# A retention kernel with two MLPs: token groups of two chunks of each sequence, shared decays, and an order of operations from a table

## Chip, cores and metric

The kernel runs on one core of a Trainium2 chip. The metric is the device time of one execution in microseconds (us), lower is better. PE is the matrix engine (PEld its weight loads), DVE the vector engine, ACT the scalar engine, POOL the GpSimd engine, SP the engine whose queue issues the DMAs here.

## What is computed

A retention layer (attention with a decaying state) for 2 sequences of 768 tokens and 8 heads of 64, then two MLPs of 512 x 2048 x 512 on the 1536 tokens, the first with a rational activation, the second with SiLU:

```python
gamma = 1.0 - 2.0 ** (-5.0 - np.arange(H))
for t in range(S):
    state = gamma[None, :, None, None] * state + np.einsum('bhd,bhe->bhde', k[:, :, t], v[:, :, t])
    y[:, :, t] = np.einsum('bhd,bhde->bhe', q[:, :, t], state) / np.sqrt(D)
x = y.transpose(0, 2, 1, 3).reshape(B * S, H * D)
h = x @ w_in; h2 = h * h
g = (a[0] + a[1] * h + a[2] * h2 + a[3] * h2 * h) / (1.0 + np.abs(b[0]) * np.abs(h) + np.abs(b[1]) * h2 + 1e-6)
x = g @ w_out
h = x @ w_in2; g = h / (1.0 + np.exp(-h))
out = g @ w_out2
```

The weights arrive as 64-bit words. The kernel makes of each a float32 (the double is put together from its two halves by integer operations) and splits it into a high and a low part, and does likewise with the activations, so that three matmuls (high x high, low x high, high x low) stand for one.

## The kernel before, in words

*Attention.* A sequence is 6 chunks of 128 tokens; `attention(c, ...)` (line 395) lists the work of one of 12 chunks. It loads kT, qT, v, k (256 KB each); multiplies k by the decay of its tokens (`kn`, POOL); computes scores (`sc`, line 417) in two PSUM banks, multiplies them by the mask on DVE (`am`); scales q by the decays `gq`, a load of 256 KB for each chunk that has a state before it (POOL, line 441); computes the growth of the state (`grow`, line 450) and the output (`outs`: line 462 within the chunk, line 472 with the state). DVE adds the growth to the state (`bd`, two buffers taken in turn, 64 x 256 twice); ACT writes the high part of the output, `xh`, and DVE the low part, `xl`. The sequence of a chunk is `divmod(c, NCI)`: chunks 0 to 5 are the first sequence, 6 to 11 the second.

*Groups.* Four chunks make a group of 512 tokens (`GT`), so there are three groups. The MLPs work on a group: 16 slices of 128 of the 2048 hidden features, two slices to a pair of weights. `use_order` (line 177) lists the uses of the pairs, 24 for the first layer and 24 for the second; a step is one slice of one group, so there are 96 steps, 48 in each layer. A step has 12 matmuls of 128x512 into a bank h (`mm_in`, line 508), the activation on ACT and DVE (11 operations in the first layer, two in the second), the split of its result into `gh` (ACT) and `gl` (POOL up to step `glp` = 21, DVE behind that), and 12 matmuls into four banks acc (`mm_out`, line 558).

*Weights.* `weights(u)` (line 332) prepares the pair of use u: four units (512 KB of raw 64-bit words each, 256 KB as float32). Of each, ACT does two activations (`wt<-raw`, `raw<-raw,par`), DVE two integer operations (line 308, `wt<-wt,raw` and `wt<-raw,wt`), ACT the high part (line 370), and POOL or DVE the low part (line 375: POOL for the first layer up to use `lop1`, for the second up to use `lop2` = 24, which is none). Four slots hold pairs, six from the end of attention on. 16 pairs are prepared from raw words and 8 brought back, as float32, from copies written to DRAM (`spill`).

*Order.* The code first lists all operations with engine, duration and rank (`op`, line 58). `Flow.order` (line 73) then plays them through engine by engine, the ready one of least rank first, and emits them in that order. The ranks come from the numbers in `R`. So every engine's queue is fixed when the kernel is built; on the chip an engine waits for the semaphores of what it needs and does nothing else meanwhile. All DMAs are issued by SP, in order.

Of the kernel before, what the change touches and what calls it, by code (L numbers as in the profile page):

```python
# [1 line left out]

# [10 lines left out]
ALU = mybir.AluOpType  # L13

P = 128
RING = 4
LATE = 2
GT = 512
UNIT = 512
R = {'T0': 321.15, 'tau0': 7.46, 'tau1': 48.5, 'c0': -178.03, 'dc': 40.95, 'conv': 16.72, 'half': 117.82, 'absl': -3.34, 'raw': 149.99, 'ret': 721.79, 'spl': 159.79, 'hi': 3.19, 'lo': -120.86, 'inn': 327.86, 'later': 56.09, 'split': 40.22, 'out': 153.78, 'evac': -230.82, 'qload': 1.4, 'scl': 120.62, 'sc': 68.71, 'am': -21.97, 'gr': 164.55, 'av': -289.58, 'bd': -408.25, 'xh': -7.59, 'xl': 65.69, 'glp': 21, 'lop1': 16, 'lop2': 24, 'scp': 0, 'ps': 18, 'ksc': 24.5, 'ka': 0, 'late': 15, 'mid': 4, 'pev': -94.54, 'pld': 38.1, 'wm': 11, 'mk': -0.34, 'ck': 14.22, 'g2': (1, 0, 2), 'lw': -276.76}  # L20
# [4 lines left out]

class Cell:


# [14 lines left out]
class Flow:  # L43
# [6 lines left out]


    TAIL = {"pe": 0.19, "act": 0.15, "dve": 0.113, "pool": 0.103, "host": 0.0}
    ISSUE, FIRST = 0.43, 2.0

# [3 lines left out]
    def op(self, eng, dur, rank, emit, reads=(), writes=(), port=False):  # L58
        after = []
        for c in reads:  # L60
            after += c.writers
        for c in writes:
            after += c.writers + c.readers
        o = Op(eng, dur, rank, emit, list(dict.fromkeys(after)), port)
        for c in reads:
            c.readers.append(o)
        for c in writes:
            c.writers, c.readers = [o], []
        o.index = len(self.ops)
        self.ops.append(o)  # L70
        return o

    def order(self):
        free = {e: 0.6 for e in (*self.TAIL, "sync")}
        cands, done = {e: [] for e in free}, []
        port = 0.0
        landed = 0.0
        for o in self.ops:
            if not o.waits:
                cands[o.eng].append(o)  # L80
        while True:
            best = None
            for e, cs in cands.items():
                if cs:
                    at = max(free[e], min(max(o.ready, port) if o.port else o.ready for o in cs))
                    if best is None or at < best[0]:
                        best = (at, e)
            if best is None:
                break
            at, e = best  # L90
            o = min(
                (o for o in cands[e] if (max(o.ready, port) if o.port else o.ready) <= at + 1e-9),
                key=lambda o: (o.rank, o.index),
            )
            cands[e].remove(o)
            o.start = at
            if e == "sync":
                free[e] = at + self.ISSUE
                landed = max(at + self.FIRST, landed) + o.dur
                end = landed + 0.1  # L100
            else:
# [12 lines left out]
        return done  # L114
# [3 lines left out]
def retention_two_mlps(  # L118
# [18 lines left out]
    B, NCI = qt.shape[:2]  # L137
# [85 lines left out]
    def at_chunk(c):  # L223
        return 5.5 * c if c < CPG else T0 + R["c0"] + R["dc"] * (c - CPG)

# [48 lines left out]
    bank = {n: Buf(n, [P, GT], F32, psum) for n in ("a0", "a1", "acc0", "acc1", "acc2", "acc3", "h0", "h1")}  # L274

# [56 lines left out]
    def weights(u):  # L332
        (l, p), s, old = loads[u]
        sl = slots[s]
        need = at_step[2 * u]
        for half in range(2):
            w = w_dram[l][half].bitcast(I32)
            nm = "io"[half]
            for un in range(2):
                rank = need - R["conv"] + R["half"] * half + un  # L340
# [5 lines left out]
                else:  # L346
# [8 lines left out]
                    dma(need - R["raw"] + half, 1.32, dst, src.rearrange("(c p) f -> p c f", p=P), [], [rh, rl])  # L355
# [26 lines left out]

    def attention(c, s_banks, o_banks):
        b, ci = divmod(c, NCI)
# [113 lines left out]
    def step(s, l, g, u, j, first, last, part):  # L498
# [43 lines left out]
        for m in range(4):  # L542
# [44 lines left out]
            elif last:  # L587
# [9 lines left out]
                r0 = g * GT + m * P  # L597
# [120 lines left out]
```

## Time and profile before

| | |
|---|---|
| time, median of 3 runs | 618.96 us (618.27 to 619.92) |
| profiled execution: its own time | 618.69 us |
| its span, first to last instruction | 616.9 us |
| mean granted TensorE clock | 0.986 |
| PE busy | 587.8 us, 95% |
| DVE busy | 441.3 us, 72% |
| ACT busy | 388.9 us, 63% |
| POOL busy | 98.2 us, 16% |
| moved by DMA | 71.34 MB |

One execution was recorded. The span is cut into 40 slices on the page: PE is at 6 to 9 tenths in the first third and at 9 or more behind it, DVE at 8 or 9 tenths from the third slice to the 27th and at 1 to 5 behind, and the DMA engines are full in the first three slices. Busy time of PE is no measure of its rate, as its instructions overlap; counts of matmuls in a window are.

### The profile page before, as it was taken

To read this page: it belongs to the slowest core of one execution; us is meant where nothing else is said; L and a number is where in the kernel's file an instruction comes from. 1 tells how busy PE (TensorE), PEld (TensorE's weight loads), DVE (VectorE), ACT (ScalarE), POOL (GpSimd) and SP (SyncE) were. 2 spreads that over 40 slices of the span, in tenths; PEclk is the share of its full clock that TensorE was granted. 3 is DMA by queue.
4 is the path that set the end of the run, shared out by engine and by line. 5 is a ranking of instruction groups with operands and counts; after the bars stand their busy time and mean duration, and the time that the engine had idled before them with its cause. 6 is when DMAs were issued, how large, how long until landed. Compare 5 with 4: busy or idle time off the path is not lost.

```text
span 616.9 us, 8056 instructions
## 1 busy us (share of the span) xinstructions
PE 587.8 (95%) x2950; PEld 477.2 (77%) x2950; DVE 441.3 (72%) x674; ACT 388.9 (63%) x657; POOL 98.2 (16%) x80
## 2 busy tenths in 40 slices
PE   6689989999989999999999999999999999999997
PEld 6577767677768788788787877877888888888886
DVE  1788998999999999999999898985424133332321
ACT  1568878898899787879788588874333132432222
POOL 1753654455443100000000000000000000000000
PEclk8988989999989999999999999999999999999999
DMA  8996774442342211004201545684122000020001
GB/s 282 384 359 210 269 255 146 156 128 75 100 150 86 70 52 35 34 1 142 98 0 52 165 156 188 208 265 162 51 86 64 6 0 26 23 73 1 0 2 68
DMA packets 34088, 71.34 MB, mean 116 GB/s; under 512 B 3712, under 2 KB 3712, under 8 KB 34048
## 3 DMA queue, kind: packets, MB, share of 16 engines
q1 hardware_dynamic: 34048, 70.82, 34.8%
q8 instruction: 23, 0.38, 0.2%
q14 instruction: 17, 0.14, 0.1%
HBM read 58.22 MB, written 12.58 MB: 115 GB/s over the span
## 4 chain that ended last, share of the span: by engine, by line
PE 32%; DVE 15%; ACT 9%; DMA 6%; issue 3%; ACTq 0%; DVEq 0%; SPq 0%
PE acc L558 17%; PE h L508 15%; DMA raw<-in_moe_w_out_dram 3%; DMA raw<-in_moe_w_in_dram 3%; DVE wt L308 2%; DVE s L308 2%; ACT r L293 2%; DVE gl L301 2%; DVE u L308 2%; DVE r L308 1%; DVE t L308 1%; ACT w L293 1%; ACT wt L293 1%; ACT s L293 1%; ACT gh L293 1%
## 5 line engine op out<-in xcount | busy, mean ns | idle before, releaser
L508 PE MATMUL h<-xh,ih 128*128 128x512 f32 x384 | 153.6, 400 | 7.1 <-DVE s L308 5.9
L508 PE MATMUL h<-xh,il 128*128 128x512 f32 x384 | 150.8, 393 | 0.3 <-DVE il L375 0.3
L508 PE MATMUL h<-xl,ih 128*128 128x512 f32 x384 | 150.5, 392 | 0.0
L301 DVE TENSOR_TENSOR gl<-w,gh 128x512 fp32r<-128x512 f32 x48 | 33.2, 691 | 104.4 <-ACT gh L293 104.4
L293 ACT ACTIVATE gh<-w 128x512 fp32r<-128x512 f32 x48 | 30.3, 631 | 104.4 <-PE acc L558 104.4
L508 PEld LDWEIGHTS h<-xh,ih 128*128 128x128 f32 x384 | 72.7, 189 | 30.2 <-DVE s L308 12.7
L508 PEld LDWEIGHTS h<-xh,il 128*128 128x128 f32 x384 | 72.5, 189 | 17.1 <-DVE il L375 1.6
L508 PEld LDWEIGHTS h<-xl,ih 128*128 128x128 f32 x384 | 72.7, 189 | 14.3
L558 PE MATMUL acc<-gh,oh 128*128 128x512 f32 x192 | 76.3, 397 | 0.0
L558 PE MATMUL acc<-oh,gh 128*128 128x512 f32 x192 | 74.8, 390 | 0.8 <-DVE xl L301 0.8
L558 PE MATMUL acc<-gl,oh 128*128 128x512 f32 x192 | 75.0, 391 | 0.0
L558 PE MATMUL acc<-gh,ol 128*128 128x512 f32 x192 | 75.0, 391 | 0.0
L558 PE MATMUL acc<-ol,gh 128*128 128x512 f32 x192 | 74.7, 389 | 0.0
L558 PE MATMUL acc<-oh,gl 128*128 128x512 f32 x192 | 74.7, 389 | 0.0
L308 DVE SCALAR_TENSOR_TENSOR wt<-raw,wt 128x512 int32<-128x512 int32 x64 | 53.6, 845 | 0.3
L308 DVE SCALAR_TENSOR_TENSOR wt<-wt,raw 128x512 int32<-128x512 int32 x64 | 46.9, 744 | 9.1 <-ACT raw L293 8.1
L293 ACT ACTIVATE wt<-raw 128x512 f32<-128x512 f32 x64 | 42.5, 667 | 16.7 <-DMA raw<-in_moe_w_in_dram 8.4
L293 ACT ACTIVATE raw<-raw,par 128x512 int32<-128x512 uint32 x64 | 48.4, 761 | 5.0 <-DMA raw<-in_moe_w_in_dram 3.3
L308 DVE SCALAR_TENSOR_TENSOR s<-s,par,h 128x512 f32<-128x512 f32 x66 | 48.9, 743 | 0.9
L308 DVE SCALAR_TENSOR_TENSOR w<-w,h 128x512 f32<-128x512 f32 x48 | 33.0, 687 | 19.2 <-ACT w L293 18.4
L558 PEld LDWEIGHTS acc<-oh,gh 128*128 128x128 f32 x192 | 36.0, 187 | 8.7 <-DVE xl L301 1.2
L558 PEld LDWEIGHTS acc<-gh,oh 128*128 128x128 f32 x192 | 36.3, 189 | 7.9
(88 smaller groups left out, 921.6 us busy)
## 6 DMA issues: line engine op xcount, KB each, us to landing
raw<-in_moe_w_in_dram SPq DMA_DIRECT2D x32, 512.0 KB, 4.0
raw<-in_moe_w_out_dram SPq DMA_DIRECT2D x32, 512.0 KB, 3.9
spill<-wt SPq DMA_DIRECT2D x32, 256.0 KB, 4.8
wt<-spill SPq DMA_DIRECT2D x32, 256.0 KB, 2.7
kT<-in_kt_dram SPq DMA_DIRECT2D x12, 256.0 KB, 5.6
qT<-in_qt_dram SPq DMA_DIRECT2D x12, 256.0 KB, 4.7
vn<-in_v_dram SPq DMA_DIRECT2D x12, 256.0 KB, 5.2
kn<-in_k_dram SPq DMA_DIRECT2D x10, 256.0 KB, 5.5
```

The costliest lines, as they stand in the source:

```text
L293: lambda: nc.scalar.activation(out=out_, in_=in_, func=func, **kw),
L301: op(eng, dur, rank, lambda: e.tensor_tensor(out=out_, in0=in0, in1=in1, op=alu), reads, writes, port)
L308: lambda: nc.vector.scalar_tensor_tensor(out=out_, in0=in0, scalar=scalar, in1=in1, op0=op0, op1=op1),
L508: nc.tensor.matmul(h.t, sl.t[w][:, ws], x[g].t[:, c, :], start=(n == 0), stop=(n == 3 * KD - 1))
L558: nc.tensor.matmul(a.t, a1, a2, start=(first and n == 0), stop=(last and n == 2))
```

## The change

- Chunk c is now sequence `c % 2`, chunk `c // 2`: a group of 512 tokens is two neighbouring chunks of each sequence. The rows of the output are put in place when they are stored.
- The decays `gq` of a chunk index are loaded once and used for both sequences (`shared`).
- Each sequence has one state buffer, updated in place.
- The order of emission is read from a packed table, `ORDER`, in place of the playing through; the ranks have no effect any more. It holds one number for each of 2124 operations.
- Of the numbers in `R`, those that still choose something have changed so: `glp` 21 to 25 (gl on POOL up to step 25), `lop2` 24 to 30 (the low parts of the second layer's pairs used at 24 to 29 on POOL), `ka` 0 to 4 (k of chunks 0 to 3 is multiplied by its decay on ACT, one activation per head, instead of on POOL), `ps` 18 to 17 (up to which step the reciprocal is kept in the bank h), `lop1` 16 to 15 and `late` 15 to 20 (no difference in what is loaded where).

The table's text, the rest of the numbers, and edits that change a rank alone are left out here:

```diff
--- before.py
+++ after.py
@@ -1,4 +1,8 @@
+import base64
+import zlib
 from contextlib import ExitStack
+
+import numpy as np
 
 import concourse.bass as bass
 import concourse.tile as tile
@@ -17,14 +21,60 @@
 LATE = 2
 GT = 512
 UNIT = 512
-R = {'T0': 321.15, 'tau0': 7.46, ... 'glp': 21, 'lop1': 16, 'lop2': 24, 'scp': 0, 'ps': 18, ... 'ka': 0, 'late': 15, 'mid': 4, ... 'wm': 11, ... 'g2': (1, 0, 2), 'lw': -276.76}
+R = {'lw': -463.92, 'T0': 689.59, 'tau0': 13.93, ... 'glp': 25, 'lop1': 15, 'lop2': 30, 'scp': 0, 'ps': 17, ... 'ka': 4, 'late': 20, 'mid': 4, ... 'wm': 11, ... 'g2': (1, 0, 2), ... 'rhalf': 125.38}
 L_SCALE = 2.0**-29 * (1.0 - 2.0**-16)
 L_BIAS = -0.5 + 7.5 * 2.0**-16
 W_SCALE = 2.0**-112
 
 
+ORDER = (
...
+)
+
+
...
@@ -47,11 +97,6 @@
 
 
 
-
-
-    TAIL = {"pe": 0.19, "act": 0.15, "dve": 0.113, "pool": 0.103, "host": 0.0}
-    ISSUE, FIRST = 0.43, 2.0
-
     def __init__(self):
         self.ops = []
 
...
@@ -71,46 +118,12 @@
         return o
 
     def order(self):
-        free = {e: 0.6 for e in (*self.TAIL, "sync")}
-        cands, done = {e: [] for e in free}, []
-        port = 0.0
-        landed = 0.0
-        for o in self.ops:
-            if not o.waits:
-                cands[o.eng].append(o)
-        while True:
-            best = None
-            for e, cs in cands.items():
-                if cs:
-                    at = max(free[e], min(max(o.ready, port) if o.port else o.ready for o in cs))
-                    if best is None or at < best[0]:
-                        best = (at, e)
-            if best is None:
-                break
-            at, e = best
-            o = min(
-                (o for o in cands[e] if (max(o.ready, port) if o.port else o.ready) <= at + 1e-9),
-                key=lambda o: (o.rank, o.index),
-            )
-            cands[e].remove(o)
-            o.start = at
-            if e == "sync":
-                free[e] = at + self.ISSUE
-                landed = max(at + self.FIRST, landed) + o.dur
-                end = landed + 0.1
-            else:
-                free[e] = at + o.dur
-                end = at + o.dur + self.TAIL[e]
-            if o.port:
-                port = at + o.dur
-            o.end = end
-            for f in o.feeds:
-                f.ready = max(f.ready, end)
-                f.waits -= 1
-                if not f.waits:
-                    cands[f.eng].append(f)
-            done.append(o)
-        assert len(done) == len(self.ops)
+        places = np.frombuffer(zlib.decompress(base64.b85decode("".join(ORDER))), np.uint16)
+        assert sorted(places) == list(range(len(self.ops)))
+        done = [self.ops[n] for n in places]
+        for n, o in enumerate(done):
+            o.place = n
+        assert all(o.place < f.place for o in done for f in o.feeds)
         return done
 
 
...
@@ -380,8 +396,10 @@
                 op("pool" if on_pool else "dve", 1.23 if on_pool else 0.6, rank + R["lo"], lo, [wt, ch], [cl], True)
 
 
+    shared = {}
+
     def attention(c, s_banks, o_banks):
-        b, ci = divmod(c, NCI)
+        ci, b = divmod(c, B)
         g, o = divmod(c, CPG)
         rank = at_chunk(c)
         more, grows = ci > 0, ci < NCI - 1
@@ -433,15 +451,15 @@
                 port=False,
             )
 
-        old = bd[(c - 1) % 2]
+        old = new = bd[b]
         if more:
 
-            gq = load(0.5, gqs, decays[ci - 1])
+            gq = shared[ci] if ci in shared else load(0.5, gqs, decays[ci - 1])
+            shared[ci] = gq
             eng = "dve" if c < R["scp"] else "pool"
             tt(eng, rank - R["scl"], qT.t[:], qT.t[:], gq.t[:], ALU.mult, [gq], [qT])
 
 
-        new = bd[c % 2]
         st, xo = bank[o_banks[0]], bank[o_banks[1]]
 
         def grow():
@@ -488,7 +506,7 @@
                 if not more:
                     act(rank + R["bd"], new.t[js, :, js], sv[js], AF.Copy, [st], [new], True, n=HP * D)
                 else:
-                    tt("dve", rank + R["bd"], new.t[js, :, js], sv[js], old.t[js, :, js], ALU.add, [st, old], [new], n=HP * D, port=False)
+                    tt("dve", rank + R["bd"], new.t[js, :, js], sv[js], new.t[js, :, js], ALU.add, [st], [new], n=HP * D, port=False)
         cols = slice(o * P, (o + 1) * P)
         hi, lo = xh[g].t[:, :, cols], xl[g].t[:, :, cols]
         act(rank + R["xh"], hi, heads(xo.t), AF.Copy, [xo], xh[g].chunk[o], True)
@@ -594,7 +612,8 @@
                     [a],
                     [o],
                 )
-                r0 = g * GT + m * P
+                ci, b = divmod(g * CPG + m, B)
+                r0 = (b * NCI + ci) * P
                 op(
                     "sync",
                     0.8,
```

## Rows read from the trace of the kernel before

**Rows 1.** The page, part 1: busy us, share of the span, instructions

```profile
PE 587.8 (95%) x2950; PEld 477.2 (77%) x2950; DVE 441.3 (72%) x674; ACT 388.9 (63%) x657; POOL 98.2 (16%) x80
```

**Rows 2.** The chain that ended last: start us, us, what

```profile
589.55 5.44 PE acc L558 x24
...
597.71 15.65 PE acc L558 x69
```

**Rows 3.** Windows of line 508: stretch, us, PE busy (matmuls); clock, DMA share, GB/s

```profile
36.00:180.00 144.00, 59.18 (x238) 0.96 0.54 178
...
300.00:420.00 120.00, 61.00 (x253) 1.00 0.46 147
```

**Rows 4.** The same for line 558 alone (`mm_out`)

```profile
36.00:180.00 144.00, 48.16 (x192) 0.96 0.54 178
...
300.00:420.00 120.00, 60.18 (x255) 1.00 0.46 147
```

**Rows 5.** PE in order of time: start, us, line, tiles, count [idle before <-releaser]

```profile
30.44 0.32 PE L462 MATMUL h<-u,vn 128*64 128x128 f32 x1 [1.98 <-DVE xl L301]
...
35.78 0.50 PE L508 MATMUL h<-xh,ih 128*128 128x512 f32 x1 [0.55 <-DVE xl L301]
...
66.03 0.69 PE L450 MATMUL a<-vn,kn 128*64 128x64 f32 x16
66.55 1.04 PE L462 MATMUL a<-am,vn 128*64 128x128 f32 x16
67.52 1.16 PE L472 MATMUL a<-qT,bd 128*128 128x128 f32 x8
...
75.49 1.16 PE L417 MATMUL a<-qT,kT 64*128 64x128 f32 x16
```

**Rows 6.** Windows: stretch, us; busy (x) PE PEld DVE ACT POOL; clock, DMA, GB/s

```profile
15.00:30.00 15.00, 9.52 (x144) 8.11 (x144) 11.09 (x17) 9.26 (x18) 11.16 (x9) 1.00 1.02 381
30.00:45.00 15.00, 14.01 (x120) 11.53 (x120) 13.24 (x19) 8.33 (x15) 8.84 (x8) 0.89 1.03 377
...
60.00:180.00 120.00, 111.73 (x646) 88.15 (x646) 112.43 (x163) 101.52 (x174) 59.77 (x45) 0.97 0.48 158
...
300.00:420.00 120.00, 117.27 (x508) 94.36 (x507) 109.95 (x177) 96.32 (x163) 0.00 (x0) 1.00 0.46 147
```

**Rows 7.** DVE in order of time, late: start us, us, what

```profile
392.93 0.68 DVE L301 TENSOR_TENSOR gl<-w,gh 128x512 fp32r<-128x512 f32 x1
393.53 0.69 DVE L375 TENSOR_TENSOR il<-wt,ih 128x512 fp32r<-128x512 f32 x1
```

**Rows 8.** DVE in order of time

```profile
9.22 1.29 DVE L301 TENSOR_TENSOR am<-a,msk 128x512 f32<-128x512 f32 x2 [7.80 <-DMA msk<-in_consts_dram]
...
27.69 1.65 DVE L308 SCALAR_TENSOR_TENSOR wt<-raw,wt 128x512 int32<-128x512 int32 x1
...
29.71 0.67 DVE L301 TENSOR_TENSOR xl<-h,xh 128x512 fp32r<-128x512 f32 x1
```

**Rows 9.** POOL in order of time

```profile
24.36 1.27 POOL L375 TENSOR_TENSOR il<-wt,ih 128x512 fp32r<-128x512 f32 x1
...
27.07 1.72 POOL L375 TENSOR_TENSOR il<-wt,ih 128x512 fp32r<-128x512 f32 x1
28.76 1.72 POOL L301 TENSOR_TENSOR qT<-qT,gq 128x512 f32<-128x512 f32 x1
```

**Rows 10.** ACT in order of time

```profile
6.55 0.29 ACT L293 ACTIVATE u<-u,par 128x1 f32<-128x1 f32 x1 [3.76 <-PE h L625]
14.88 0.60 ACT L293 ACTIVATE xh<-h 128x512 fp32r<-128x512 f32 x1 [8.04 <-PE h L462]
...
18.66 0.38 ACT L293 ACTIVATE bd<-h 64x256 f32<-64x256 f32 x1 [2.35 <-PE h L450]
```

**Rows 11.** The page, part 5: busy us, mean ns | idle before, releaser

```profile
L308 DVE SCALAR_TENSOR_TENSOR wt<-raw,wt 128x512 int32<-128x512 int32 x64 | 53.6, 845 | 0.3
L308 DVE SCALAR_TENSOR_TENSOR wt<-wt,raw 128x512 int32<-128x512 int32 x64 | 46.9, 744 | 9.1 <-ACT raw L293 8.1
```

More of the change, by code (lines that the diff above doesn't have):

```diff
@@ L19 @@
 UNIT = 512
-R = {'T0': 321.15, 'tau0': 7.46, 'tau1': 48.5, 'c0': -178.03, 'dc': 40.95, 'conv': 16.72, 'half': 117.82, 'absl': -3.34, 'raw': 149.99, 'ret': 721.79, 'spl': 159.79, 'hi': 3.19, 'lo': -120.86, 'inn': 327.86, 'later': 56.09, 'split': 40.22, 'out': 153.78, 'evac': -230.82, 'qload': 1.4, 'scl': 120.62, 'sc': 68.71, 'am': -21.97, 'gr': 164.55, 'av': -289.58, 'bd': -408.25, 'xh': -7.59, 'xl': 65.69, 'glp': 21, 'lop1': 16, 'lop2': 24, 'scp': 0, 'ps': 18, 'ksc': 24.5, 'ka': 0, 'late': 15, 'mid': 4, 'pev': -94.54, 'pld': 38.1, 'wm': 11, 'mk': -0.34, 'ck': 14.22, 'g2': (1, 0, 2), 'lw': -276.76}
+R = {'lw': -463.92, 'T0': 689.59, 'tau0': 13.93, 'tau1': 122.19, 'c0': -129.63, 'dc': 67.51, 'conv': 39.61, 'half': 427.29, 'absl': -34.77, 'raw': 455.03, 'ret': 752.06, 'spl': -417.39, 'hi': 301.24, 'lo': 31.56, 'inn': -277.93, 'later': -32.81, 'split': -554.53, 'out': 359.39, 'evac': -363.13, 'qload': -20.08, 'scl': 238.79, 'sc': 858.37, 'am': -44.15, 'gr': 112.48, 'av': -547.62, 'bd': 198.47, 'xh': -201.14, 'xl': 110.32, 'glp': 25, 'lop1': 15, 'lop2': 30, 'scp': 0, 'ps': 17, 'ksc': 103.89, 'qa': -467.29, 'ka': 4, 'late': 20, 'mid': 4, 'pev': -317.29, 'pld': -385.01, 'cg': -489.85, 'wm': 11, 'mk': 26.43, 'ck': 21.3, 'g2': (1, 0, 2), 'ch0': 269.21, 'ch1': -102.81, 'ch2': 64.3, 'ch3': 22.33, 'ch4': -52.46, 'ch5': 5.42, 'ch6': -78.23, 'ch7': 237.84, 'ch8': 90.06, 'ch9': -61.88, 'ch10': -106.39, 'ch11': -212.52, 'ru0': 218.22, 'lu0': -107.8, 'ru1': 40.68, 'lu1': -106.06, 'ru2': 91.09, 'lu2': 146.01, 'ru3': -37.17, 'lu3': -39.51, 'rhalf': 125.38}
 L_SCALE = 2.0**-29 * (1.0 - 2.0**-16)
@@ L26 @@
 class Cell:
+    bank = None
     def __init__(self):
@@ L64, in op @@
         o = Op(eng, dur, rank, emit, list(dict.fromkeys(after)), port)
+        banks = [c.bank for c in (*reads, *writes) if c.bank is not None]
+        o.bank = banks[0] if banks and eng in ("act", "dve") else None
         for c in reads:
@@ L223, in at_chunk @@
     def at_chunk(c):
-        return 5.5 * c if c < CPG else T0 + R["c0"] + R["dc"] * (c - CPG)
+        return R[f"ch{c}"] + (5.5 * c if c < CPG else T0 + R["c0"] + R["dc"] * (c - CPG))
     cst = Buf("cst", [P, NGAM])
@@ L274, in retention_two_mlps @@
     bank = {n: Buf(n, [P, GT], F32, psum) for n in ("a0", "a1", "acc0", "acc1", "acc2", "acc3", "h0", "h1")}
+    for n, x in enumerate(bank.values()):
+        x.bank = n
     at_stack = ExitStack()
@@ L334, in weights @@
         sl = slots[s]
-        need = at_step[2 * u]
+        need, early = at_step[2 * u], R.get(f"ru{u}", 0.0)
         for half in range(2):
@@ L339, in weights @@
             for un in range(2):
-                rank = need - R["conv"] + R["half"] * half + un
+                rank = need - R["conv"] + early + R["half"] * half + un
                 us = slice(un * UNIT, (un + 1) * UNIT)
@@ L354, in weights @@
                     dst = raw.t[:].rearrange("p (c f) t -> p c (f t)", c=c)
-                    dma(need - R["raw"] + half, 1.32, dst, src.rearrange("(c p) f -> p c f", p=P), [], [rh, rl])
+                    dma(need - R["raw"] + R.get(f"lu{u}", 0.0) + half * R["rhalf"], 1.32, dst, src.rearrange("(c p) f -> p c f", p=P), [], [rh, rl])
                     wi = wt.t.bitcast(I32)
```

40 lines of the change are left out of this document (added).

## The prediction

> **What bounds the kernel now.** I begin with the page's first part: PE is busy 95% of the span, DVE 72%, ACT 63%, POOL 16% [rows 1]. A busy PE is not a PE at its peak, so its real rate is needed. In the chain of work that ended last, a run of 24 MLP matmuls takes 5.44 us, one after the other, 226.7 ns a matmul [rows 2]. The kernel has 96 steps of 24 matmuls each: 96 x 5.44 = 522 us that no reordering removes. The span is 616.9 us, so 95 us are something else. The question is where they lie.
>
> The windows of the two MLP lines tell it. Between 36 and 180 us there are 238 + 192 = 430 matmuls, 97.5 us of MLP work in 144 us [rows 3, 4]. Between 300 and 420 us there are 253 + 255 = 508, 115.2 us of 120. Behind that it is all PE: the chain is runs of 5.44 us up to its last run, which ends at 613.36 [rows 2]. Nothing can be won in the last third.
>
> The first MLP matmul starts at 35.78 us [rows 5]. What runs before is attention on the first 512 tokens and the loads. A chunk of attention costs PE 1.16 (scores) + 0.69 (state) + 1.04 and 1.16 (output) = 4.0 us where a state exists, some 3.7 with the overlap of the pipeline [rows 5]; seven and a half chunks stand between 36 and 180, 28 us. So 144 - 97.5 - 28 = 18.5 us of that stretch is waiting or slow clock (the mean granted clock there is 0.96, so a part of it ran at 1.2 GHz; it is 1.00 in 300 to 420 [rows 3]).
>
> What holds PE up early? From 15 to 45 us the DMA engines are busy for the whole of the time at 377 to 381 GB/s [rows 6]: 256 KB lands every 0.69 us and 512 KB every 1.38. From 60 to 180 it is DVE, 112.4 of 120 us busy, with POOL at 59.8 [rows 6]. From 300 to 420 DVE is still at 110 of 120, POOL at nothing.
>
> Two more readings are needed. First, a DVE instruction that has others queued behind it costs 0.60 us, not the 0.69 of its bar: two neighbours start 0.60 apart [rows 7]. Second, DVE and POOL get in each other's way. A DVE instruction with all its operands in SBUF that began at 27.69 took 1.65 us; the POOL instruction beside it ran from 27.07 to 28.79, and DVE ended 0.55 after that. A DVE instruction that reads PSUM took its ordinary 0.67 at 29.71, beside a POOL instruction from 28.76 to 30.48 [rows 8, 9].
>
> **The change, part by part.** The table is a packed list of 16-bit places. Unpacked and held against the order in which the code lists its operations, it gives the queue of every engine. Against the kernel before, the work is this: SP issues 5 loads of decays fewer. 28 subtractions go from DVE to POOL: 24 low parts of second-layer weights (pairs used at 24 to 29) and 4 of gl (steps 22 to 25). Four multiplications of k go from POOL to ACT, 8 small activations each. PE has the same operations.
>
> *The start.* A group of 512 tokens was four chunks of one sequence, each of which needs the state behind the one before; now it is two chunks of each of two sequences. The first of each has no state, and the group needs one load of decays where it needed three. In the table PE has 16 items ahead of the first MLP matmuls: all of chunks 0 to 3, and chunk 4 as a whole. SP's list up to the last load that these need: four of 256 KB and two small ones, then the mask (before, it came behind four of 256 KB too, and DVE began at 9.22, when it had landed [rows 8]); I put it at 9.9 for the small ones. Behind it stand 24 units of 256 KB up to chunk 4's v, and chunk 3's v is unit 22: 9.9 + 22 x 0.69 = 25.1, and 26.5 for chunk 4. From 25.1: the output matmuls 2.2, ACT's high part 0.60 [rows 10], DVE's low part 0.69, hand-offs 0.3 give 28.9; the state matmuls of chunks 3 and 4 and chunk 4's outputs, which PE does in between, give 25.1 + 2.2 + 0.7 + 0.7 + 2.2 = 30.9. I take 30.9. That is 4.9 us ahead of 35.78, and chunk 4's outputs (2.2 us), which came behind the first matmuls, are done: a lead of 7.1.
>
> ACT could spoil it. Nothing of before shows an activation of 128x64 with a pointer for its scale. One of 128x1 with a pointer took 0.29, one of 64x256 without took 0.38 [rows 10]; less up to 0.09 for the overlap of neighbours (that of DVE's [rows 7]), 32 of them cost 6.4 to 9.3 us at 0.20 to 0.29, and 12.2 at 0.38. The 128x1 is nearer to 64 elements: 0.25 each, 2.0 us a chunk. Ahead of the high part of chunk 3 ACT has four of these, a table load of 1.3 and 17 other activations of 0.3 to 0.7: 8.0 + 1.3 + 8.5 = 17.8. Starting near 7 us, when the first k and the factors of the decay have landed, that is 24.8, before the 27.3 at which the output of chunk 3 is ready. So it hides, with 2.5 us to spare; if each costs 0.29 it is 1.3 us later and still hides. I take 1 us off the lead for waits that the count does not see: **-6.0 us**, with the bounds 0 (if DVE and ACT rather than the loads end the chain, as at 30.44, where PE waited 1.98 for DVE [rows 5]) and -9.
>
> *The five loads.* 5 x 0.69 = 3.4 us of the DMA pipe. What of it counts lies before 45 us and is in the term above; later the DMA engines are half idle [rows 3], and it is worth nothing.
>
> *36 to 180 us.* The work of DVE, POOL and PE is that of before; only its order differs. The lead is kept as long as DVE and PE stay as full as they were. Of the 18.5 us lost there a better order could win perhaps 12 (clock and unavoidable hand-offs keep the rest); a worse one could lose a third, 6. No row says which: I take 0.
>
> *The subtractions on POOL.* DVE is relieved of 28 x 0.60 = 16.8 us, 14.4 of it in the stage around 300 to 420. There POOL gets 24 x 1.27 = 30.5 us [rows 9]. Between the last DVE operations of steps 45 and 60 the table has 87 of DVE (52 us), 17 of which read PSUM, 19 of POOL (24 us) and 72 us of PE. If every POOL instruction lies beside DVE instructions that read PSUM or beside idle time, DVE needs 66 us and PE sets the pace; if none does, 76 and hand-offs, and DVE sets it. In before's early stage the two stretched forms average 845 and 744 ns against 687: 64 x (158 + 57) ns = 13.8 us over 76 POOL instructions (the 80 of [rows 1] less four that set constants), 0.18 each [rows 11]. There 59 of the first 207 DVE operations (28%) had no PSUM operand; here 80% have none, so I scale: 0.18 x 0.80/0.28 = 0.5 us each, 12 us on 24, and with the late POOL results about what DVE was relieved of. Value **0**; bounds: a gain of 4.8 (120 - 115.2, all that PE loses in 300 to 420), a loss of 16 (30.5 - 14.4, nothing covered). The Trainium skill's page "SBUF — State Buffer", section "Who interferes with whom", speaks against this part: a DVE instruction with two SBUF inputs and a GpSimd instruction that reads SBUF exclude each other for their whole length. By that rule, with no cover, the estimate is the 16 us of loss; the pair at 27.07 and 27.69 agrees with it [rows 8, 9].
>
> The state in place and the rows of the output change no instruction's size: nothing.
>
> *Sum.* The profiled execution took 618.69 us, 616.9 of it span, and lies 0.27 under the median of 618.96. 618.69 - 6.0 + 0 + 0 + 0 = 612.7; against the median, **613.0 us**.
>
> **The rivals.** (a) *The order also fills the middle.* The two independent sequences leave DVE fewer moments without a ready instruction, and half to two thirds of the 18.5 us go too: 613 - 9 = 604. For it: the waits are of PE on DVE, DVE on ACT. Against: DVE's 112 of 120 us leaves it 8.
> (b) *The lead is given back.* DVE has the same work up to step 31, and if it, not PE, sets the pace from 36 us on, its own start counts: first work at 9 to 10 us in both. Then only DVE's gaps before 45 us are won, under 2 us: 618.
> (c) *Slower: the port.* From pair 24 on, POOL's 24 subtractions take the place of DVE's as the thing weights wait for. Priced at 16 x 0.8 = 13 us (the fifth that reads PSUM covers its share), less the lead of 6: 619 + 7 = 626. It decides where more than half of the POOL time (12 of 24 us between steps 45 and 60) finds a DVE instruction without a PSUM operand next in the queue. For it: 80% of them are such. Against: DVE had 10 us idle there to give [rows 6].
> (d) *The loads are not what is late at the start*, so that fewer and reordered ones bring nothing: the first MLP matmul is again at 35 to 36 us, which gives (b)'s time.
>
> **How the numbers follow.** The forecast (606 to 616.5) has 0.44, (a) 0.20, (b) and (d) 0.16, (c) 0.20. A measurement of this kernel can tell about 0.3%, 1.9 us, from no change. Faster: 0.44 + 0.20 = 0.64. Same: 0.16. Slower: 0.20. For the range I leave out the lower third of (a) and the upper half of (c): 601 to 624.
>
> **What would show it.** The first MLP matmul at 29 to 32 us, with chunk 4's output before it, and the mask's landing near 10: the start. DVE's share between 60 and 180 unchanged: the lead is carried. In 300 to 420, POOL at 24 to 30 us, DVE instructions of 1.2 to 1.9 us beside it, and MLP matmuls per 120 us near 508: the late term; under 490 would be (c). The prediction is wrong if ACT's small activations cost over 0.4 us, if PE waits for ACT before 30 us, or if the step pace between 36 and 180 changes by more than 5 us.

## The result: 599.6 us, and the profile after

The changed kernel takes 599.61 us (median; 597.68 to 600.01) against 618.62 (618.27 to 619.92) for the kernel before on the same chip: a ratio of 0.968, with a 95% interval of 0.9657 to 0.9709. The forecast was 613.0, with a range of 601 to 624. The direction was right; the gain, 19 us, is three times the 6 us of the sum. The profiled execution took 599.9 us, 598.1 of it span.

The page of after, part 1 (answers to [rows 1]: busy us, share of the span, instructions):

```profile
PE 579.3 (97%) x2950; PEld 475.6 (80%) x2950; DVE 426.7 (71%) x646; ACT 396.9 (66%) x690; POOL 134.8 (23%) x104
```

28 instructions left DVE and 24 net came to POOL, as the sum had it. DVE's share hardly moved, since the span shrank too.

Windows of all engines, after (answers to [rows 6]: stretch, us, then busy us and instructions of PE, PEld, DVE, ACT, POOL, then clock, DMA share, GB/s):

```profile
15.00:30.00 15.00, 12.09 (x192) 10.46 (x190) 11.79 (x20) 11.82 (x31) 8.59 (x7) 0.97 0.94 326
30.00:45.00 15.00, 12.74 (x126) 10.36 (x121) 13.68 (x25) 11.13 (x21) 6.75 (x6) 1.00 0.93 329
...
60.00:180.00 120.00, 119.81 (x679) 96.92 (x679) 112.84 (x174) 108.75 (x185) 60.44 (x46) 1.00 0.44 149
...
300.00:420.00 120.00, 118.45 (x519) 96.97 (x519) 101.51 (x142) 89.93 (x153) 34.91 (x23) 1.00 0.55 171
```

The row to look at is the third. Between 60 and 180 us PE's busy time went from 111.73 to 119.81 us and its clock from 0.97 to 1.00. DVE was busy for 112.4 us before and for 112.8 now, POOL for 59.8 and 60.4: neither had less to do there. But DVE started 174 instructions where it had started 163, and ACT 185 where it had 174.

Windows of the two MLP lines, after: first line 526 (`mm_in`; answers to [rows 3]), then line 576 (`mm_out`; [rows 4]); columns as there.

```profile
36.00:180.00 144.00, 63.05 (x264) 49.04 (x264) 0.99 0.52 179
300.00:420.00 120.00, 62.82 (x264) 49.10 (x263) 1.00 0.55 171
```

```profile
36.00:180.00 144.00, 54.97 (x223) 41.28 (x224) 0.99 0.52 179
300.00:420.00 120.00, 60.51 (x255) 47.88 (x256) 1.00 0.55 171
```

36 to 180 us now holds 487 MLP matmuls, where it held 430; 300 to 420 holds 519, where it held 508.

To see where the 19 us came from, I count PE's work at its own rate from the records of both traces: 226.7 ns for an MLP matmul, and for an attention matmul the time to the next one, at most 150 ns. That sum, at five moments:

| by | before, us of work (MLP matmuls) | after | lead of after | gained in the stretch |
|---|---|---|---|---|
| 36 us | 19.6 (1) | 23.5 (12) | 3.9 | 3.9 |
| 60 us | 38.2 (49) | 41.6 (53) | 3.4 | -0.5 |
| 180 us | 141.1 (430) | 157.5 (499) | 16.4 | 13.0 |
| 300 us | 258.8 (949) | 275.2 (1018) | 16.4 | 0.0 |
| 420 us | 373.7 (1456) | 392.6 (1536) | 18.9 | 2.5 |

So 13 of the 19 us come from the stretch that the sum had put at nothing.

What PE waited for between 60 and 180 us, first before, then after (engine, tile, line, releaser: us in total, times, longest):

```profile
PE h L508 <- DVE s L308: 3.8, 4, 1.9
PE a L450 <- DVE am L301: 2.1, 1, 2.1
PE a L462 <- DVE am L301: 1.2, 2, 0.9
PE a L417 <- ACT bd L293: 0.6, 1, 0.6
PE a L417 <- DVE bd L301: 0.5, 1, 0.5
```

```profile
PE a L480 <- DVE am L317: 0.2, 1, 0.2
```

8.2 us of waits became 0.2. Nearly all of them were for results of DVE, an engine that was busy for 112.4 of the 120 us. One of them in full, before, DVE and then PE in order of time:

```profile
74.67 2.38 DVE L308 SCALAR_TENSOR_TENSOR wt<-raw,wt 128x512 int32<-128x512 int32 x2
76.98 0.74 DVE L308 SCALAR_TENSOR_TENSOR u<-w,par,h 128x512 f32<-128x512 f32 x1
77.63 0.68 DVE L301 TENSOR_TENSOR s<-s,h 128x512 f32<-128x512 f32 x1
78.34 0.75 DVE L308 SCALAR_TENSOR_TENSOR s<-s,par,h 128x512 f32<-128x512 f32 x1
79.66 0.75 DVE L308 SCALAR_TENSOR_TENSOR u<-w,par,h 128x512 f32<-128x512 f32 x1 [0.57 <-ACT s L293]
80.32 1.28 DVE L301 TENSOR_TENSOR am<-a,msk 128x512 f32<-128x512 f32 x2
```

```profile
78.53 0.39 PE L558 MATMUL acc<-gl,oh 128*128 128x512 f32 x1
81.06 0.69 PE L450 MATMUL a<-vn,kn 128*64 128x64 f32 x16 [2.14 <-DVE am L301]
81.66 1.18 PE L462 MATMUL a<-am,vn 128*64 128x128 f32 x16
82.77 2.08 PE L472 MATMUL a<-qT,bd 128*128 128x128 f32 x8
```

The scores that `am` masks were done at 76.65 (75.49 + 1.16 [rows 5]). DVE finishes a pair of weight operations, one of them lengthened (2.38 us for two), does three operations of an MLP step, waits 0.57 us for ACT with a `u` at the head of its queue, does that `u`, and only then `am`, at 80.32. PE stands for 2.14 us. Then its clock falls: eight matmuls that take 1.16 us elsewhere [rows 5] take 2.08, and the window behind shows a granted clock of 0.57, near the lower level of 1.2 GHz:

```profile
82.00:86.00 4.00, 4.00 (x26) 3.45 (x23) 3.73 (x8) 3.46 (x7) 0.00 (x0) 0.57 0.50 183
```

The mean granted clock was 0.57 in these 4 us and 0.66 from 174 to 179, behind a wait of 1.95 us; PE was busy all through both, so that before lost 1.7 us in each to the clock, 3.4 between 60 and 180 us, and after nothing. Waits and clock, 8.0 + 3.4, are 11.4 of the 13 us.

The four waits for `s` (3.8 us) are less plain. The longest of them, the 1.95 us, ended at 173.41, when DVE had done the `s` that it had begun at 172.60. Ahead of that, DVE had done four weight operations from 162.44 to 166.03, had waited 0.57 us for ACT and had done one more weight operation at 169.90; the rest was the work of the MLP steps itself.

### The profile page after: what moved, and what is told of

Its sections match the earlier page's. It is cut to its first block, busy times and chain, and to the rows that moved or that the text cites. A ratio compares the mean times of both kernels' runs of the same rounds, so it can differ in the third digit from the quotient of the medians.

```text
span 598.1 us, 8106 instructions
## 1 busy us (share of the span) xinstructions
PE 579.3 (97%) x2950; PEld 475.6 (80%) x2950; DVE 426.7 (71%) x646; ACT 396.9 (66%) x690; POOL 134.8 (23%) x104
## 4 chain that ended last, share of the span: by engine, by line
PE 57%; DVE 17%; DMA 13%; ACT 9%; issue 2%; SPq 2%; ACTq 0%; DVEq 0%
PE acc L576 28%; PE h L526 27%; DMA raw<-in_moe_w_in_dram 6%; DVE wt L324 4%; DVE s L324 3%; DMA raw<-in_moe_w_out_dram 3%; DMA spill<-wt 2%; SPq L343 2%; DVE s L317 2%; DVE gl L317 1%; ACT wt L309 1%; ACT raw L309 1%; DVE u L324 1%; DVE t L324 1%; DVE r L324 1%
## 5 line engine op out<-in xcount | busy, mean ns | idle before, releaser
L526 PE MATMUL h<-xh,ih 128*128 128x512 f32 x384 | 150.7, 392 | 2.2 <-DVE s L324 1.9
L317 DVE TENSOR_TENSOR gl<-w,gh 128x512 fp32r<-128x512 f32 x48 | 34.2, 712 | 82.5 <-ACT gh L309 82.4
L391 POOL TENSOR_TENSOR ol<-wt,oh 128x512 fp32r<-128x512 f32 x28 | 40.0, 1431 | 119.3 <-ACT oh L386 114.9
L324 DVE SCALAR_TENSOR_TENSOR wt<-wt,raw 128x512 int32<-128x512 int32 x64 | 50.4, 796 | 10.4 <-ACT wt L309 5.7
L309 ACT ACTIVATE w<-h 128x512 f32<-128x512 f32 x48 | 28.3, 593 | 35.9 <-PE h L526 25.0
L317 POOL TENSOR_TENSOR gl<-s,gh 128x512 fp32r<-128x512 f32 x26 | 35.2, 1356 | 69.9 <-ACT gh L309 47.0
```

Of the source, the lines that this page charges most:

```text
L309: lambda: nc.scalar.activation(out=out_, in_=in_, func=func, **kw),
L317: op(eng, dur, rank, lambda: e.tensor_tensor(out=out_, in0=in0, in1=in1, op=alu), reads, writes, port)
L324: lambda: nc.vector.scalar_tensor_tensor(out=out_, in0=in0, scalar=scalar, in1=in1, op0=op0, op1=op1),
L391: e.tensor_tensor(out=sl.t[nm + "l"][:, us], in0=wt.t, in1=sl.t[nm + "h"][:, us].bitcast(F32), op=ALU.subtract)
L526: nc.tensor.matmul(h.t, sl.t[w][:, ws], x[g].t[:, c, :], start=(n == 0), stop=(n == 3 * KD - 1))
```

## The experiments

Three theories. **A**: the order in the table makes the gain. **B**: the new chunks (groups of both sequences, shared decays) make it. **C**: the relief of DVE (work moved to POOL and ACT) makes it. The ratios are to the kernel before on the same chip, whose median was 617.7 to 618.6. The runs were spread over several chips, so a difference between two rows is surer by the ratios than by the times. "By 180" is the count of MLP matmuls that PE has started by then in the one profiled execution, which in e10 (650.7 us) and e11 (606.0) was the slowest of its six.

| kernel | us | ratio, 95% interval | first MLP matmul | by 60 | by 180 | by 420 |
|---|---|---|---|---|---|---|
| before | 618.6 | 1 | 35.8 | 49 | 430 | 1456 |
| after | 599.6 | 0.966 to 0.971 | 31.9 | 53 | 499 | 1536 |
| e1 new chunks, old order | 633.4 | 1.019 to 1.028 | 34.2 | 45 | 396 | 1404 |
| e2 and the moved work | 635.2 | 1.023 to 1.030 | 37.4 | 24 | 392 | 1396 |
| e3 table to 60 us, old order behind | 630.3 | 1.012 to 1.022 | 33.8 | 48 | 447 | 1407 |
| e4 old order to 60 us, table behind | 617.2 | 0.996 to 1.000 | 34.9 | 24 | 420 | 1461 |
| e5 low parts back on DVE | 600.2 | 0.968 to 0.973 | 32.2 | 47 | 492 | 1535 |
| e6 decays of k back on POOL | 601.1 | 0.970 to 0.975 | 32.0 | 52 | 498 | 1538 |
| e7 five loads back | 599.4 | 0.967 to 0.972 | 30.7 | 56 | 505 | 1544 |
| e8 old chunks, table's order | 608.0 | 0.982 to 0.987 | 32.2 | 36 | 463 | 1503 |
| e9 DVE neighbours exchanged | 608.0 | 0.980 to 0.988 | 31.6 | 57 | 474 | 1508 |
| e10 before with the moved work | 646.9 | 1.044 to 1.050 | 44.6 | 24 | 339 | 1326 |
| e11 four gl back on DVE | 602.6 | 0.972 to 0.978 | 33.4 | 44 | 487 | 1509 |
| e12 before, POOL cut | 611.2 | 0.986 to 0.992 | 34.7 | 54 | 467 | 1495 |
| e13 after, POOL cut | 595.9 | 0.963 to 0.967 | 30.0 | 60 | 507 | 1555 |
| e14 e9, POOL cut | 602.3 | 0.974 to 0.980 | 31.6 | 55 | 483 | 1529 |

### One part alone: e1 and e2

e1 is after with the table taken out again: the order is worked out as in before, with before's ranks and its division of work.

```diff
-R = {... 'glp': 25, 'lop1': 15, 'lop2': 30, ... 'ps': 17, ... 'ka': 4, ...}
+R = {... 'glp': 21, 'lop1': 16, 'lop2': 24, ... 'ps': 18, ... 'ka': 0, ...}
-        places = np.frombuffer(zlib.decompress(base64.b85decode("".join(ORDER))), np.uint16)
-        done = [self.ops[n] for n in places]
+        (the playing through of before, by ready time and rank)
```

> The changed kernel's chunks (two of each sequence to a group, decays loaded once for both, state in place), but the operations are put in order by the playing-through of the kernel before with its ranks and its split of work between the engines (glp 21, lop2 24, ka 0, ps 18). Theory A (the table's order is what gained 19 us, above all in 60 to 180 us): 610 to 618 us, at most the gain of the start, 4 us, and some loss because the ranks were not made for these chunks; DVE instructions of more than 850 ns in 60 to 180 us stay near 12, PE loses 12 to 17 us there. Theory B (the chunks gained it, since two sequences give every engine something to do): 600 to 606 us, with the MLP matmuls of 60 to 180 us as many as in the changed kernel.

e2 is e1 with `glp` 25, `lop2` 30 and `ka` 4.

> The same as the one before it, and the work is split as in the changed kernel: 24 low parts of weights and 4 of gl on POOL instead of DVE, k of chunks 0 to 3 multiplied on ACT. Only the table is missing. Theory A (order): 608 to 618, within 4 us of the one before it. Theory C (the relief of DVE gained it): 600 to 606, at least 8 us under the one before it. If the moved work costs by the port, as the prediction's rival (c) has it: 620 or more.

633.4 and 635.2 us: the new chunks alone, and the chunks with the moved work, are 15 and 17 us slower than before. B and C fall as causes that work by themselves. A's ranges (610 to 618 and 608 to 618) are missed too, by 15 and 17 us: that these parts would cost so much without the order, no theory said. e2 lies in the range for the port (620 or more), but e1, without the moved work, is as slow within 2 us. The ranks of before were chosen for its own chunks, so e1 doesn't say that the new chunks are bad; it says that they bring nothing without an order made for them. e1's waits between 60 and 180 us are before's, only larger:

```profile
PE h L521 <- DVE s L319: 12.6, 5, 5.5
```

### Half of the table: e3 and e4

e3 takes the first 330 places of the table (to about 60 us) and plays the rest through in the old way; e4 orders the same 330 operations in the old way and takes the rest from the table. Both have before's ranks and after's division of work.

```diff
+CUT = 330
+HEAD_BY_TABLE = True        (e4: False)
+        table = [self.ops[n] for n in places]
+        head = table[:CUT]
```

> The changed kernel with the first 330 of its 2124 operations in the table's order (what runs up to about 60 us) and the rest by the playing-through of before. Theory A in the form that the middle's order matters: the start is as in the changed kernel (first MLP matmul near 31.9 us), then 8 to 16 us are lost again in 60 to 180: 608 to 615. If a good start alone sets the pace of all that comes: 599 to 603.

> The reverse: the first 330 operations of the table (the same set) in the order of the playing-through of before, the rest by the table. Theory A in the form that the middle's order matters: only the start's 4 us are lost, 602 to 606. If the start sets the pace: 608 to 616.

e3 begins like after and then falls back: 447 MLP matmuls by 180, 960 between 180 and 420 where after has 1037. e4 begins worse than before (24 by 60 us), and its start goes on costing behind the 330 places: between 60 and 120 us PE does 47.8 us of work, by the count that gave the 13 us, where after does 56.5. From 120 to 420 us it runs like after (294.8 and 294.5). So the half ordered in the old way costs 31 us in e3 and 18 in e4, with the chunks and the division of work of after in both: the order matters, in both halves, which is A in its main point. Its sizes were wrong. It had put e3 at 608 to 615 us and e4 at 602 to 606; the rival that the start sets the pace had e4 at 608 to 616, and e4 is beyond that as well.

### The moved work undone: e5, e6, e11 and e7

Four kernels change one thing in after and leave the rest of its order (e7 takes the operations by their place in the table, each as soon as what it depends on is listed, to fit in its five loads):

```diff
-'lop2': 30    'ka': 4    'glp': 25
+'lop2': 24                              (e5)
+              'ka': 0                   (e6)
+                         'glp': 21      (e11)
-            gq = shared[ci] if ci in shared else load(0.5, gqs, decays[ci - 1])
+            gq = load(0.5, gqs, decays[ci - 1])       (e7)
```

> The kernel after with one number changed: 24 of the low-part subtractions go back from GpSimd to VectorE (lop2 30 to 24), in the same order. Theory A (the order of the table made the gain): the table was made for the other engine, so VectorE gets some 14 us more work, most of it after 240 us, where TensorE loses under 4 us in all: 600 to 606 us. Theory C (the relief of VectorE is what brings the gain): 608 us or more. Rival, the predicted price of the subtractions on GpSimd (12 us of stretch against 14.4 us of relief): within 2 us of the kernel after, either way, and stretched VectorE instructions between 300 and 420 us fall from 16 to near 0.

> The kernel after with the key decays back on GpSimd instead of ScalarE (ka 4 to 0), in the same order. Theory A: the decays are late in nothing that TensorE waits for, so within 2 us of the kernel after (598 to 602 us). Rival (ScalarE's taking them is what lets the middle of the kernel run): 604 us or more, with TensorE's lost time between 60 and 180 us back above 8 us, and more stretched VectorE instructions there than the 5 of after.

> The kernel after with four of the products' low parts back on VectorE (25 to 21 on GpSimd), as in before, in the same order. Theory A: within 2 us of the kernel after (598 to 602 us). Rival (GpSimd's extra share is what frees VectorE in the middle): 604 us or more, with TensorE's lost time between 60 and 180 us above 8 us.

> The kernel after with an own load of the decays for every chunk again: five DMAs more on SyncE's queue, each behind its chunk's query load. Theory A: no difference that can be measured (598 to 602 us, first MLP matmul at 31.9 us give or take 0.5). Rival (the shared loads are the gain at the start, since the DMA share is full there): first MLP matmul 1 to 2 us later and the time 601 to 603 us.

e5 and e7 can't be told from after. e6 is 1.5 us above it at the median (2.7 by the ratios), with intervals that overlap. e11 is 3 us above (4.2 by the ratios), with an interval of its own, and misses the 2 us of A. At the place of its four products PE waits twice for `s`, 1.4 us in all between 180 and 240 us, where after doesn't. The rest of its lag is there by 60 us (44 matmuls to 53), where these products change nothing; profiled runs of kernels with this order had 44 to 57 by then (e5, e6, e7, e9, e11), so that part I put down to no cause. C is refuted as the cause of the 19 us: no part of the moved work, put back alone, takes more than 3 to 4 of them away. All parts together were not put back in this order. And the price of 0 for the 24 low parts holds: e5's longer DVE instructions between 300 and 420 us vanish, and the time stays.

### The order with the moves, and the moves alone: e8 and e10

e8 has before's chunks, loads and states and after's division of work, and takes the operations by their place in the table, each as soon as what it depends on is listed:

```diff
-        ci, b = divmod(c, B)
+        b, ci = divmod(c, NCI)
-        old = new = bd[b]
+        old, new = bd[(c - 1) % 2], bd[c % 2]
+        prio = {int(n): k for k, n in enumerate(table)}
+            _, n = heapq.heappop(ready)
```

> The chunks, their decays and the state as in the kernel before (one chunk of each sequence in a group, an own load of decays for each, a new state tile each time), but the order of all operations from the table of the kernel after, as near as the dependences let it, with after's division between the engines. Theory A in its strong form (the order alone): 599 to 605 us. Theory A in its weak form (the order fits only the new chunks): 605 to 615 us, with the loss at the start, first MLP matmul above 33 us. Theory B (the new chunks are what pays): 615 us or more, TensorE losing over 8 us between 60 and 180 us again.

608.0 us, A in its weak form in size (605 to 615), though the first MLP matmul came at 32.2, not above 33. The order, with the division of work that it was made for, wins 9.8 us of the 19 without the new chunks. From 60 us on e8 keeps nearly after's pace (427 MLP matmuls between 60 and 180, with half a chunk more of attention to do, where after has 446 and before 381); it lies behind because it enters with 36 where after has 53. That deficit is the worth of the new chunks within this order, about 8 us, or of how badly the table fits the old ones: e8 doesn't part the two, and a few matmuls of it are the spread of starts seen above.

e10 is the other half of that pair, before with `glp` 25, `lop2` 30 and `ka` 4 and its own way of ordering.

> The kernel before, its chunks, loads, states and its own order worked out at build time, with only the division of work changed: 30 instead of 24 low parts and 25 instead of 21 subtractions on GpSimd, four key decays on ScalarE. Theory C (the relief of VectorE pays): 610 us or less. Theory A: no gain without the order: 616 to 622 us, with some 12 us of VectorE stretch after 300 us where before had none. My predicted price of the subtractions (nothing, bounds -4.8 to +16 us) covers both.

646.9 us, 29 us slower, which no theory had expected. PE and DVE between 60 and 180 us, windows with the columns of [rows 6]:

```profile
60.00:180.00 120.00, 105.46 (x637) 84.12 (x636) 102.85 (x146) 88.10 (x150) 54.76 (x40) 0.91 0.47 152
```

DVE has less to do in the whole, and is busy for less of this stretch: 102.9 us and 146 instructions, where before had 112.4 and 163. It waits (10.8 us for ACT's `s`, 9 times), and PE waits for it (10.0 us for `s`). Moving work between engines upset the order that the old way of ordering arrived at, by far more than the work was worth. e8 has the same chunks and the same division of work as e10 but for `ps`, `lop1` and `late`; between these two the order is worth 39 us.

### What in the order: e9

e9 leaves the table coarsely as it is. Between places 330 and 763 (about 60 to 180 us) each pair of neighbouring DVE operations that don't depend on each other is exchanged; the other engines' orders stay.

```diff
+        queue = [o for o in done if o.eng == "dve" and LO <= o.place < HI]
+            if all(o.place < a.place for o in before[id(b)]) and all(f.place > b.place for f in a.feeds):
+                a.place, b.place = b.place, a.place
```

> The kernel after with its table disturbed finely: between places 330 and 763 of the order (about 60 to 180 us) every pair of neighbouring VectorE operations that doesn't depend on each other is exchanged; every other engine's order stays. Theory A1 (the gain between 60 and 180 us is a coarse one: what is prepared ahead of what): within 2 us of the kernel after (598 to 602 us), TensorE's lost time between 60 and 180 us under 6 us of the 20.8 of before 60 to 240... stated plainly: 4.1 us in after, under 6 here. Theory A2 (it is a fine one: which VectorE operation runs beside which of GpSimd's): stretched VectorE instructions there rise from 5 (1.8 us) towards the 12 (9.3 us) of before, and the time is 603 to 610 us.

608.0 us: moving DVE operations by one place costs 8.4 us (9.7 by the ratios), 25 matmuls (5.7 us) of it by 180 us in the profiled run. PE's waits for DVE and DVE's for ACT between 60 and 180 us, the longest of each (after had 0.2 us on PE in all, and on DVE 2.4 us, 2 times, for the first of its rows):

```profile
PE h L541 <- DVE s L339: 4.0, 5, 1.8
PE a L450 <- DVE bd L332: 0.7, 1, 0.7
```

```profile
DVE t L339 <- ACT h L324: 4.7, 7, 1.4
DVE u L339 <- ACT s L324: 1.3, 2, 0.6
```

That is what A2 said of the time. Of A2's mechanism, DVE instructions running long beside POOL, it shows only a part: I count 8 DVE instructions of over 850 ns there (4.9 us beyond an ordinary length), where after has 5 (1.8 us) and before 12 (9.3 us). DVE's idle time rose as much, from 7.2 to 10.9 us.

### POOL's length, or the order of DVE's results: e12, e13 and e14

P says: the gain is fewer DVE instructions held up by POOL. Q says: it is DVE's results coming in the order in which PE needs them. Three kernels take POOL's long subtractions away, down to 16 of 512 columns, in before, after and e9.

```diff
+                    m = 16 if e is nc.gpsimd and key in written else UNIT
+                if eng == "pool" and id(out_) in written:
+                    m = 16
```

> The kernel before in its own order, with GpSimd's subtractions (the weights' low parts and the products' low parts) done for 16 of 512 columns, except the first into each buffer: most of the low parts are left out, the operations and their order stay. Theory P (what before loses between 60 and 180 us is lost to VectorE instructions that run long beside GpSimd): stretch there falls from 9.3 us to 3 or less and the time to 604 to 611 us. Theory Q (it is lost to the order in which VectorE's results come): 614 to 619 us.

> The kernel after with the same cut of GpSimd's subtractions to 16 of 512 columns. Both theories: little to gain, since TensorE loses 4.1 us between 60 and 180 us and 5 us after it: 594 to 600 us. The difference to the cut kernel before is the test: under 10 us by P (19 without the cut), 14 us or more by Q.

> The kernel after with VectorE's independent neighbours exchanged between about 60 and 180 us, and the same cut of GpSimd's subtractions. Without the cut the exchange cost 8 us. Theory P: with the cut it costs under 3 us. Theory Q: 5 us or more remain.

The cut brings 6.8 us in before, 3.7 in after, 5.7 in e9 (6.8, 2.3 and 4.5 by the ratios). The lengthening went as intended (1.5 us left between 60 and 180 in e12, of 9.3). The kernels before and after still lie 15.2 us apart, where Q said 14 or more; e12's 611.2 falls between the two theories' ranges, at the edge of P's. The exchange of neighbours still costs 6.4 us of 8.4, where Q said 5 or more.

The 15.2 us can't be put down to Q as a whole, though. They hold the start (3.7 us of PE's work by 60 us) and 300 to 420 us (4.3), and both theories speak of 60 to 180. There the cut kernels e12 and e13 do 110.2 and 116.2 us of PE's work, 6.0 apart, where before and after did 102.9 and 115.9, 13.0 apart. So in the profiled executions about half of what the order won in this stretch goes with POOL's long subtractions, as P says, and about half stays, as Q says. e9's loss there falls from 6.4 us to 4.2 (e14). Windows of e12 and then e13, columns of [rows 6]:

```profile
60.00:180.00 120.00, 115.61 (x679) 91.97 (x678) 110.50 (x173) 107.01 (x185) 29.95 (x47) 1.00 0.50 168
```

```profile
60.00:180.00 120.00, 119.89 (x681) 97.28 (x680) 112.24 (x174) 108.87 (x186) 27.51 (x46) 1.00 0.43 145
```

With POOL cut and its own order, before's DVE starts 173 instructions there, after's 174: the 11 that it lacked were lost to the lengthening. The clock stays at 1.00, so the 3.4 us that it cost go with the cut too. What is left is waits: 4.0 us of PE for DVE in e12, none in e13. P's half is work of the order too, since POOL is as busy in this stretch in before as in after; which instructions run side by side is what differs. The cut also brings POOL's results earlier, which these runs don't part from P.

With POOL out of the way, before's DVE still waits for `s` from ACT; this row is e12's, 60 to 180 us (before had 4.7 us, 8 times, for the same; e13 has 0.4, once):

```profile
DVE u L324 <- ACT s L293: 6.9, 11, 1.5
```

In total after's DVE waits about as long as before's did (5.4 and 5.9 us). What differs is that PE then doesn't stand behind it.

Of the kernels that leave nothing out, none is faster than after by more than the intervals can tell.

## Why the prediction was wrong, and where it was right

*The bound*, right. The MLP still runs at 5.44 us for 24 matmuls, and nothing moved behind 420 us.

*The start*, -6.0, inside its bounds but too large: measured -3.9 at 36 us and -3.4 at 60. The first MLP matmul was put at 30.9 and came at 31.86, behind chunk 4's outputs as the table's order said; the mask, put at 9.9, let DVE begin at 9.37. PE in order of time, after (answers to [rows 5]):

```profile
29.97 1.05 PE L480 MATMUL a<-am,vn 128*64 128x128 f32 x16
30.95 1.16 PE L490 MATMUL a<-qT,bd 128*128 128x128 f32 x8
31.86 0.47 PE L526 MATMUL h<-xh,ih 128*128 128x512 f32 x1
```

The sum counted chunk 4's outputs as 2.2 us of lead on top of the time. By 31.86 us after had done 20.4 us of attention, before by 35.78 had done 19.4: the real surplus was 1.0, since before had pulled other pieces of attention forward. e7 shows that the five loads cost nothing, at the start either: with them put back the first matmul comes at 30.7. Rival (d) was right in that premise, and wrong in concluding that the start then stays where it was. And e8, with the old chunks, has it at 32.2. So what I gave as the reason of the early start (no chain of states, fewer loads) isn't needed for it; the order, with its division of work, is enough. In e8 the lead was gone by 60 us (35.7 us of work, before 38.2).

*ACT's small activations*, right in size: estimated at 0.25 us each, measured at 3.92 for 16, 0.245. They didn't hide as counted: PE waited 1.38 us for the first `kn` and 0.69 for a `bd` of ACT, both before 30 us, which the prediction had named as a sign of being wrong. ACT did two table loads of 1.28 us by 13.3 us, where the sum had one. The waits cost the start nothing that shows, as e6, with `kn` on POOL, has its first MLP matmul at 32.0.

```profile
8.03 3.92 ACT L421 ACTIVATE kn<-kn,cst 128x64 f32<-128x64 f32 x16
```

```profile
10.34 2.14 PE L468 MATMUL h<-vn,kn 128*64 128x64 f32 x16 [1.38 <-ACT kn L421]
25.17 0.69 PE L468 MATMUL h<-vn,kn 128*64 128x64 f32 x16 [0.69 <-ACT bd L309]
```

*36 to 180 us*, put at 0 with bounds of -12 and +6: the step that failed. It measured -12.5 (-13.0 from 60 to 180 alone), beyond the better bound; the step pace there changed by more than the 5 us that the prediction had named as a sign of being wrong. The sentence "No row says which: I take 0" is where it went wrong, and so is rival (a)'s counterargument, "DVE's 112 of 120 us leaves it 8". A busy share isn't work done. DVE's 112 us held 9.3 us of lengthening, after 1.8, and within the same busy time it later did 11 instructions more; e12 shows that the lengthening was what held these up. And PE's 8 us of waits there were nearly all for DVE, one of them at least for a result that DVE had queued behind other work (the row at 81.06); to queue it otherwise costs DVE no work. Half of the gain in the stretch is the one and half the other, as far as e12 and e13 tell, and both came from the order. The rows were to be had: of PE's nine waits between 60 and 180 us eight name DVE, and the one at 81.06 shows on DVE, in the rows ahead of `am`, what was done first. The table could have been held against these places, as I held it against the start. Rival (a) named the effect, at 604 and a chance of 0.20; its reason, two independent sequences, isn't the main one, since e8 keeps most of the pace in the middle with the old chunks.

*The subtractions on POOL*, put at 0 with 12 us of lengthening: DVE's instructions of 300 to 420 us were lengthened by 12.6 us (16 of over 850 ns, beside 23 of POOL), where before had none. The price was right too: e5 undoes it and the time stays. POOL's 23 took 34.9 us, 1.52 each, where the sum had 1.27 each and the sign of it had 24 to 30 us: POOL's own instructions were lengthened as well. But the bound of +16 and rival (c) asked the wrong thing: DVE's idle time there rose from 10.1 to 18.5 us all the same, so it had the room. A pair of them, DVE and POOL:

```profile
331.90 1.78 DVE L324 SCALAR_TENSOR_TENSOR s<-s,par,r 128x512 f32<-128x512 f32 x1
```

```profile
331.46 1.66 POOL L391 TENSOR_TENSOR ol<-wt,oh 128x512 fp32r<-128x512 f32 x1 [4.30 <-issue]
```

The DVE instruction, an ordinary 0.74 us one at 330.03, ends 0.56 us behind POOL's. The Trainium skill's page "SBUF — State Buffer", section "Who interferes with whom", says that a DVE instruction with two SBUF inputs and a GpSimd instruction that reads SBUF exclude each other. The trace agrees: 1.78 us here where an ordinary one takes 0.74. The 16 us of loss worked out from it didn't come. PE started 519 MLP matmuls in these 120 us, where before had 508 and e13, with POOL cut, 530: what the lengthening held up PE by is some 2.5 us there (11 matmuls).

That term missed by the 2.5 us won between 300 and 420 us. No run separates what in the order brings them; e5, without the 24 subtractions on POOL, has them too (1043 matmuls between 180 and 420, after 1037, before 1026).

*What stays open.* How much of the 8 us between e8 and after belongs to the new chunks, and how much to the table not being made for the old ones. What the table's order of ACT, PE, POOL and the loads is worth apart from DVE's: e9 moved DVE's alone, and no run moved that of another engine alone. The split of the middle between P and Q rests on one profiled execution of each kernel.

## What to carry to other kernels

Where PE waits for an engine that is busy nearly all the time, look at what that engine did in the few instructions ahead of the late one: if that wasn't due yet, the wait belongs to the order, and a new order can win it back with every engine's work as it was. Look also for instructions that run long beside another engine's; here the order decided how many did. A busy share says how long an engine was occupied, so compare instructions started in equal windows as well. Data layout, division of work and order are one change: here the chunks without the order cost 15 us, the moved work without it 29, and with both together, and an order made for them, the kernel won 19.

## What the runs showed of the hardware beyond that

PE's waits can cost more than their length: the lower clock behind a wait of 2.14 us made eight matmuls 0.92 us longer and lasted into the next ones. The mean granted clock between 60 and 180 us was lowest where PE waited most for DVE: 0.91 in e10 (14.3 us of such waits), 0.96 in e1 (14.2), 0.97 in before (7.6), 1.00 in after (0.2). The sum of the waits doesn't settle it: e9 kept 1.00 with 4.7 us of them, e12 with 4.0, and e3 had 0.97 with 4.9.
